# Attention scores from plain float32 queries and keys of 64 rows per head, in place of stacked high and low float32r parts

## The chip, the cores and the metric

One core of one Trainium2 chip runs the whole program in one launch. The metric is the time on the device in microseconds, the median of several runs.

## The reference

Three layers follow one another: attention over 4 batches x 8 heads (576 positions, 64 channels per head) with rotated queries and keys, a key/value layer with a gate, and a mixer over tokens and channels. What matters here is the first, cut to its core:

```python
def _attn_ref(q, k, v):                       # [4, 8, 576, 64]
    def rotate(x):
        x1, x2 = (x[..., :half], x[..., half:])
        return np.concatenate([x1 * cos - x2 * sin, x1 * sin + x2 * cos], axis=-1)
    q_rot, k_rot = (rotate(q), rotate(k))
    scores = scale * np.matmul(q_rot, k_rot.transpose(0, 1, 3, 2))     # scale = 1/8
    scores = scores - np.max(scores, axis=-1, keepdims=True)
    attn = np.exp(scores)
    attn = attn / (np.sum(attn, axis=-1, keepdims=True) + 1e-09)
    return np.matmul(attn, v).astype(np.float32)
```

The two layers behind it are products with weights w_k, w_v and w_r (the key/value and gate part) and w_tok1, w_tok2, w_ch1 and w_ch2 (the mixer).

## The kernel before

Heads are taken in pairs, A and B: 16 pairs in all, the 64 channels of A on partitions 0 to 63 and those of B on 64 to 127. A pair has nine score tiles, `TILES`: four of 128 queries for A, four for B, and R with the last 64 queries of both. Each tile has 576 scores per query, in two halves of 288 columns. 144 steps (`a_step`) go through the tiles one by one, in a pipeline: scores of tile i+1 on TensorE (`emit_S`), its maximum on VectorE (`emit_max`, L389), exponential of tile i on ScalarE (`emit_exp`, L396), then division into a high float16 part on ScalarE (`emit_hi`, through L75) and a low one on VectorE (`emit_lo`, L420), a transpose by DMA (`emit_tr`, L436 to L444) and the products with the values (`emit_pv`, L455), four units per pair. The score tiles have two buffers in PSUM (`S_p`).

`prep` does the work for the pairs to come, beside the steps: it loads keys and queries (`ld_raw`, L262, six buffers) and the values, rotates keys and queries on GpSimd in place (`rope`, two multiplications with the table `tab` and an addition; the first pair partly on VectorE), and scales the values (`v_max` to `v_shift`; its small products `vps` at L316 and L337 are plain float32, one row or one column wide, one call of each per pair).

TensorE takes float32r at a coarser precision than float32, so operands come in two parts: a high one, rounded, and a low one, the rest. For the scores `split_hi` copies the rounded keys and queries (the latter with the factor 1/8) on ScalarE (L73 and L75), and `split_lo` subtracts: keys on GpSimd (L297, through the helper at L104), queries on VectorE (L301). The two parts of the keys of one head are stacked on 128 partitions (`kst`: high on one half, low on the other), and each part of the queries stands on both halves (`qst`), which a DMA at L305 brings about (a ScalarE copy for the first pair). So one product over 128 rows does two of the four partial products, and a score tile takes four products (two parts of the queries, two halves of the columns); tile R, which takes both heads into one accumulation with zeros beside them, takes eight.

In the first four pairs VectorE also converts weights of the next layer (`Conv`, L201 to L207); from the fifth on the key/value products of the batch before (`kvr_gen`, `mm3`, L569 to L571, tiles kp and vp, 288 columns) run beside attention, ten of them per step (`KVN`, twice). The rest of that layer, the gate and the mixer come behind attention. The order on each engine is made by a scheduler from the program's order and the priorities in `PRI`; all DMAs are issued by SyncE.

Of the kernel before, what the change touches and what calls it, by code (L numbers as in the profile page):

```python
# [19 lines left out]
QW = 640  # L20
# [4 lines left out]
# float64 words as float32: the high word of float32's least and largest exponents  # L25
F64_LEAST = struct.unpack("<f", struct.pack("<I", 0x38000000))[0]
F64_MOST = struct.unpack("<f", struct.pack("<I", 0x47EFFFFF))[0]
# score tiles of a pair of heads: 128 queries of A or B; R: the last 64 of both
TILES = ["A0", "A1", "A2", "A3", "R", "B2", "B3", "B0", "B1"]
NT = len(TILES)  # L30
# steps, relative to a pair's first, of its four units of attention times value
PV_AT = {7: (0, 0), 10: (0, 1), 12: (1, 0), 13: (1, 1)}
# key/value and gate parts that run beside one another once attention is done with all but the last batch
SEQ = [("K", 3, 0), ("R", 0, 0), ("R", 0, 1), ("K", 3, 1)]
# how far each stream of work is taken at a time
KVN, TKN, PRE, PRE_EARLY, PRE_FROM = 5, 6, 20, 6, 6
# buffers of the pools of the first part
BUFS = dict(raw=6, vr=2, v16=2, e=7, p16=3, pt0=1, pt1=2, tm=2, sm=4, sc=3, la=1, lf=1, xs=4, t=2, q=2, vt=2)
# how much earlier than in the program's order the scheduler takes a kind of work
# [25 lines left out]
def body(tc, qk, vw, tabs, ident, mu, w_k, w_v, w_r, w_t1, w_t2, w_c1, w_c2, out):  # L65
# [18 lines left out]
    class ahead:  # L84
        """earlier (or, below 0, later) in the scheduler's order than in the program's"""
# [21 lines left out]
    with ctx:  # L107
# [10 lines left out]
        # ---------------------------------------------------------------- key/value/gate work and weights  # L118
# [7 lines left out]
        class Weights:  # L126
            """pieces of weights in a pool: each one's float64 words, then in their place its two float32r parts"""
# [28 lines left out]
        def behind(o, name):  # L156
            """keeps an instruction behind the latest of that name in their engine's order"""
            if name in last:
                tc.add_manual_dep(o.ins, last[name].ins.name, mybir.DependencyInfo(
                    mybir.DependencyClass.NoSync, mybir.DependencyReason.DATA), reason="order")  # L160

        class Conv:
            """splits weights piece by piece; the stages of successive pieces overlap"""
# [50 lines left out]
            def step(self):  # L214
                """two pieces further"""
                n = self.n
                self.n += 2
                with ahead(PRI.get(self.name, 0)):
                    for j in (3, 2, 1, 0):
                        for fs in zip_longest(*(self.stage(j, n + d - 2 * j) for d in range(2))):  # L220
                            for f in fs:
                                if f is not None:
                                    f()

        # ---------------------------------------------------------------- attention
# [11 lines left out]
        st_p = right("st", 1)  # L237
# [10 lines left out]
        tab = tab_p.tile([128, 2, S], F32, name="tab")  # L248

        raw_t, v_t, v16_t, sc_t = {}, {}, {}, {}  # L250
        # per head: [high; low] parts of the keys (low; high for the second), the queries' parts on both halves
        kst = [st_p.tile([128, S], F32R, name=f"kst{x}") for x in range(2)]
        qst = [st_p.tile([128, 2, QW], F32R, name=f"qst{x}") for x in range(2)]
# [20 lines left out]
        def rope(g, j, k, e):  # L274
            t = raw_t[g][j]
            if k < 2:
                o = tt(e, t[k], t[k], tab[:, k], ALU.mult)
# [4 lines left out]

        @prio("qk")
        def split_hi(g, x, j, e):
            l = slice(64 * x, 64 * x + 64)
            t = raw_t[g][j][0][l]
            if j == 0:
                copy(e, kst[x][l], t)
            else:
                copy(e, qst[x][l, 0, 64 * x:64 * x + S], t, 0.125)  # L290

        @prio("qk")
        def split_lo(g, x, j, e="P"):
            l, o = slice(64 * x, 64 * x + 64), slice(64 - 64 * x, 128 - 64 * x)
            t = raw_t[g][j][0][l]
            if j == 0:
                tt(e, kst[x][o], t, kst[x][l].bitcast(F32), ALU.subtract)  # L297
                return
            c = slice(64 * x, 64 * x + S)
            lo, hi = qst[x][l, 1, c], qst[x][l, 0, c].bitcast(F32)  # L300
            dve.scalar_tensor_tensor(out=lo, in0=t, scalar=0.125, in1=hi, op0=ALU.mult, op1=ALU.subtract)  # L301
            if g == 0:
                copy("A", qst[x][o, :, c], qst[x].bitcast(F32)[l, :, c])
            else:
                sp.dma_start(qst[x].bitcast(F32)[o, :, c], qst[x].bitcast(F32)[l, :, c])  # L305
# [14 lines left out]
        def v_pow(g):  # L320
            """a power of two that brings the values near float16's largest, and what undoes it"""
# [48 lines left out]
        def emit_S(i):  # L370
            n = TILES[i % NT]
            p = S_p.tile([128, 2, 512], F32, tag="S", name="S")
            parts = []
            for x, nm in enumerate("AB"):
                if n == "R":
                    parts.append((x, 512 if x == 0 else 0))
                elif n[0] == nm:
                    parts.append((x, 128 * int(n[1]) + 128 * x))
            for j, (x, c) in enumerate(parts):
                for s in range(2):  # L380
                    for h in range(2):
                        pe.matmul(p[:, h, 0:HS], lhsT=qst[x][:, s, c:c + 128], rhs=kst[x][:, h * HS:(h + 1) * HS],  # L382
                                  start=(j == 0 and s == 0), stop=(j == len(parts) - 1 and s == 1))
# [63 lines left out]
        def emit_pv(g, x, u):  # L447
            """the products; returns what follows on ACT and then on DVE"""
# [32 lines left out]
        def prep(g, k):  # L481
            """work for pair g; k: step relative to the first of pair g - 1"""
# [25 lines left out]
            if k in (4, 8):  # L508
                x = k // 8
                split_hi(g, x, 0, "A")  # L510
                split_hi(g, x, 1, "A")
            elif k in (5, 9):
                x = k // 9
                split_lo(g, x, 1)
                split_lo(g, x, 0)
# [4 lines left out]
        def a_step(i, kv):  # L520
            """one step of the attention's pipeline"""
# [31 lines left out]
        # ---------------------------------------------------------------- key/value part, gate part  # L553
# [12 lines left out]
        def mm3(p, w, m, t, first, last):  # L566
            """the products of w's m-th 128 columns"""
# [5 lines left out]
        def kvr_gen(seq, ready):  # L573
            """seq: list of (kind, b, c); kind K: key and value products, kind R: gate and its product"""
# [112 lines left out]
        # ================================================================ emission  # L687
        ld_raw(0, ((0, 0),))
        sp.dma_start(tab[:, 0], tabs[:, 0])
        ld_raw(0, ((1, 0), (0, 1)))  # L690
        sp.dma_start(tab[:, 1], tabs[:, 1])
        ld_raw(0, ((1, 1),))
# [5 lines left out]
        for x in range(2):  # L698
            pool.memset(qst[x].bitcast(F32)[:, :, S - S * x:QW - S * x], 0.0)
# [6 lines left out]
        for x in range(2):  # L706
            for j in (1, 0):
                split_hi(0, x, j, "A")
                split_lo(0, x, j, "D")
            if x == 0:  # L710
                emit_S(0)
                emit_max(0)
# [39 lines left out]
        def tok_gen(b):  # L752
            """u = y + token mixing, in place of y; half of the channels at a time"""
# [43 lines left out]
        # ---- second weights  # L797
# [40 lines left out]
        # ---------------------------------------------------------------- gate and mixer  # L838
# [9 lines left out]
        def gate_gen(b):  # L848
            """y = sigmoid(r) * v, in place of v"""
# [148 lines left out]
```

## Time and profile before

| | |
|---|---|
| median of 3 runs | 1056.97 us (1056.59 to 1060.08) |
| span of the profiled execution | 1055.4 us, 1.6 us under the median |
| TensorE (PE) busy | 879.1 us, 83% |
| VectorE (DVE) busy | 709.2 us, 67% |
| ScalarE (ACT) busy | 534.9 us, 51% |
| GpSimd (POOL) busy | 509.1 us, 48% |
| mean granted TensorE clock | 0.918 |
| attention | the first 525 us |

The shares are means over stages with different bounds, so a change in one stage is read from the stretch it lies in. A busy TensorE is counted with the pipeline of its matmuls: two that overlap count until the second has ended.

### The profile page before, as it was taken

To read this page: it belongs to the slowest core of one execution; us is meant where nothing else is said; L and a number is where in the kernel's file an instruction comes from. 1 tells how busy PE (TensorE), PEld (TensorE's weight loads), DVE (VectorE), ACT (ScalarE), POOL (GpSimd) and SP (SyncE) were. 2 spreads that over 40 slices of the span, in tenths; PEclk is the share of its full clock that TensorE was granted. 3 is DMA by queue.
4 is the path that set the end of the run, shared out by engine and by line. 5 is a ranking of instruction groups with operands and counts; after the bars stand their busy time and mean duration, and the time that the engine had idled before them with its cause. 6 is when DMAs were issued, how large, how long until landed. Compare 5 with 4: busy or idle time off the path is not lost.

```text
span 1055.4 us, 16829 instructions
## 1 busy us (share of the span) xinstructions
PE 879.1 (83%) x6000; PEld 814.4 (77%) x6000; DVE 709.2 (67%) x1355; ACT 534.9 (51%) x1130; POOL 509.1 (48%) x480
## 2 busy tenths in 40 slices
PE   2354566888887897788977898889999999999998
PEld 1333345677777787677967897889999999999997
DVE  6999999898899998998798459963222312131111
ACT  3665758777776786778754254443224112211110
POOL 6765885695889774774355545451123003201010
PEclk9665668999999999899988998989999999999999
DMA  6897979999897888979880147001021002000000
GB/s 199 206 204 184 214 168 189 184 203 191 181 185 172 185 187 175 202 140 197 200 272 17 42 171 284 16 24 46 1 85 30 23 1 73 1 24 1 24 23 23
DMA packets 216371, 130.56 MB, mean 124 GB/s; under 512 B 175712, under 2 KB 191200, under 8 KB 216160
## 3 DMA queue, kind: packets, MB, share of 16 engines
q1 hardware_dynamic: 216288, 129.50, 52.1%
q8 instruction: 47, 0.77, 0.3%
q14 instruction: 36, 0.29, 0.1%
HBM read 59.79 MB, written 14.16 MB: 70 GB/s over the span
## 4 chain that ended last, share of the span: by engine, by line
PE 37%; DVE 9%; issue 2%; DMA 1%; ACT 1%; POOL 1%; SPq 0%; DVEq 0%; POOLq 0%; ACTq 0%
PE c1p L569 4%; PE co L570 4%; PE co L569 4%; PE co L571 4%; PE c1p L570 4%; PE c1p L571 4%; DVE cv L201 2%; DVE cv L205 2%; DVE cv L207 1%; PE rp L569 1%; PE rp L570 1%; PE rp L571 1%; DVE cv L203 1%; PE trp L762 1%; PE t1p L776 1%
## 5 line engine op out<-in xcount | busy, mean ns | idle before, releaser
L382 PE MATMUL S<-kst,qst 128*128 128x288 f32 x640 | 136.0, 350 | 57.3 <-ACT e L396 44.1
L382 PEld LDWEIGHTS S<-kst,qst 128*128 128x128 f32 x640 | 110.3, 226 | 70.0 <-ACT e L396 49.4
L420 DVE SCALAR_TENSOR_TENSOR p<-e,rc,p 128x576 f16<-128x576 f32 x144 | 156.2, 1090 | 11.3 <-ACT p L75 10.8
L902 DVE SCALAR_TENSOR_TENSOR hs<-c1p,hs 128x288 fp32r<-128x288 f32 x96 | 43.5, 454 | 151.1 <-ACT hs L901 150.6
L75 ACT ACTIVATE p<-e,rc 128x576 f16<-128x576 f32 x144 | 110.1, 771 | 65.2 <-DMA pt<-p 30.8
L455 PE MATMUL pv<-pt,v 128*128 128x256 f16 (+1 forms) x576 | 97.2, 317 | 39.3 <-DMA pt<-p 34.6
L396 ACT ACTIVATE e<-S,nm 128x576 f32<-128x576 f32 x144 | 105.8, 735 | 44.5 <-DVE nm L389 43.3
L104 POOL TENSOR_TENSOR raw<-raw,tab 128x576 f32<-128x576 f32 x62 | 103.4, 1677 | 48.1 <-DMA raw<-in_qk_dram 47.8
L901 ACT ACTIVATE hs<-c1p 128x288 fp32r<-128x288 f32 x96 | 38.7, 408 | 170.0 <-PE c1p L571 166.4
L104 POOL TENSOR_TENSOR uhl<-y,uhl 128x288 fp32r<-128x288 f32 x32 | 25.8, 836 | 194.1 <-ACT uhl L73 194.1
L569 PE MATMUL c1p<-uhl,parts 128*128 128x288 f32 x384 | 116.0, 303 | 3.6 <-DVE hs L902 3.0
L571 PE MATMUL c1p<-uhl,parts 128*128 128x288 f32 x384 | 115.0, 300 | 0.1
L570 PE MATMUL c1p<-uhl,parts 128*128 128x288 f32 x384 | 114.9, 300 | 0.0
L570 PE MATMUL co<-hs,parts 128*128 128x288 f32 x384 | 113.3, 297 | 0.0
L571 PE MATMUL co<-hs,parts 128*128 128x288 f32 x384 | 113.0, 297 | 0.0
L389 DVE TENSOR_REDUCE nm<-S 128x1 f32<-128x576 f32 x144 | 107.2, 745 | 6.2 <-PE S L382 5.1
L569 PE MATMUL co<-hs,parts 128*128 128x288 f32 x384 | 109.7, 300 | 0.7 <-ACT hs L901 0.5
L455 PEld LDWEIGHTS <-v 128*128 128x128 f16 x576 | 55.4, 106 | 65.6 <-issue 29.5
L104 POOL TENSOR_TENSOR parts<-cv,parts 128x512 fp32r<-128x512 f32 (+2 forms) x51 | 73.5, 1441 | 56.8 <-ACT parts L73 54.5
L569 PE MATMUL kp<-xs,parts 128*128 128x288 f32 x256 | 80.5, 322 | 13.2 <-ACT vt L73 6.9
L569 PE MATMUL vp<-k,parts 128*128 128x288 f32 x256 | 78.2, 312 | 3.1 <-DVE k L80 1.5
L570 PE MATMUL kp<-xs,parts 128*128 128x288 f32 x256 | 79.4, 311 | 0.3 <-POOL xs L104 0.2
(111 smaller groups left out, 2527.8 us busy)
## 6 DMA issues: line engine op xcount, KB each, us to landing
raw<-in_qk_dram SPq DMA_DIRECT2D x64, 288.0 KB, 4.0
words<-in_w_c_dram SPq DMA_DIRECT2D x24, 512.0 KB, 8.3
qst<-qst SPq DMA_DIRECT2D x30, 288.0 KB, 3.7
vr<-in_vw_dram SPq DMA_DIRECT2D x16, 320.0 KB, 4.0
xd<-xT SPq DMA_DIRECT2D x16, 288.5 KB, 2.8
vd<-vt SPq DMA_DIRECT2D x32, 144.0 KB, 2.4
y<-vd SPq DMA_DIRECT2D x8, 576.0 KB, 5.7
out_dram<-y SPq DMA_DIRECT2D x8, 576.0 KB, 3.5
```

The lines of the kernel that those rows point to most:

```text
L75: act.activation(out=o, in_=i, func=AF.Copy, scale=scale)
L104: return (pool if e == "P" else dve).tensor_tensor(o, a, b, op=op)
L382: pe.matmul(p[:, h, 0:HS], lhsT=qst[x][:, s, c:c + 128], rhs=kst[x][:, h * HS:(h + 1) * HS], start=(j == 0 and s == 0), stop=(j == len(par ...
L389: dve.tensor_reduce(out=nm, in_=S_t[i][:, :, 0:HS], op=ALU.max, axis=AX.XY, negate=True)
L396: act.activation(out=e, in_=S_t.pop(i)[:, :, 0:HS], func=AF.Exp, bias=sum_t[i][:, 0:1], accum_out=s)
L420: dve.scalar_tensor_tensor(out=t[:, S:2 * S], in0=e_t.pop(i), scalar=sum_t.pop(i)[:, 0:1], in1=t[:, 0:S], op0=ALU.mult, op1=ALU.subtract)
L455: pe.matmul(p[:, 0:n], lhsT=vt[:, j, 128 * x:128 * x + 128], rhs=t[:, j, :], start=(j == 0), stop=(j == 8))
L569: pe.matmul(p, lhsT=wh, rhs=t[:, 0], start=first, stop=False)
L570: pe.matmul(p, lhsT=wh, rhs=t[:, 1], start=False, stop=False)
L571: pe.matmul(p, lhsT=wl, rhs=t[:, 0], start=False, stop=last)
L901: act.activation(out=h[:, 0], in_=p[:, 0:HS], func=AF.Relu)
L902: dve.scalar_tensor_tensor(out=h[:, 1], in0=p[:, 0:HS], scalar=0.0, in1=h[:, 0].bitcast(F32), op0=ALU.max, op1=ALU.subtract)
```

## The change

The queries and keys are no longer split. After the rotation, which now brings the factor 1/8 into the queries by a second pair of tables, a score product takes the 64 rows of a head as they are, in float32. A tile takes two products, R four (64 queries of A to the upper half of the output, 64 of B to the lower). `split_hi`, `split_lo`, `kst` and `qst` go, with the DMA between the halves and the memory they took; the loads have ten buffers in place of six, since keys and queries are now read until their pair's last tile. The table at the start is twice as large and is loaded in two parts, that for the keys first. All else is as before (the rest of the diff takes out comments).

```diff
-BUFS = dict(raw=6, ...
+BUFS = dict(raw=10, ...
...
-        st_p = right("st", 1)
-        tab = tab_p.tile([128, 2, S], F32, name="tab")
+        tab = tab_p.tile([128, 4, S], F32, name="tab")
-        kst = [st_p.tile([128, S], F32R, name=f"kst{x}") for x in range(2)]
-        qst = [st_p.tile([128, 2, QW], F32R, name=f"qst{x}") for x in range(2)]
...
-                o = tt(e, t[k], t[k], tab[:, k], ALU.mult)
+                o = tt(e, t[k], t[k], tab[:, 2 * j + k], ALU.mult)
...
-        def split_hi(g, x, j, e):
...
-        def split_lo(g, x, j, e="P"):
...
         def emit_S(i):
             n = TILES[i % NT]
             p = S_p.tile([128, 2, 512], F32, tag="S", name="S")
-            parts = []
+            g = i // NT
+            k, q = raw_t[g][0][0], raw_t[g][1][0]
             for x, nm in enumerate("AB"):
                 if n == "R":
-                    parts.append((x, 512 if x == 0 else 0))
+                    c, w, o = (512, 64, 0) if x == 0 else (0, 64, 64)
                 elif n[0] == nm:
-                    parts.append((x, 128 * int(n[1]) + 128 * x))
-            for j, (x, c) in enumerate(parts):
-                for s in range(2):
-                    for h in range(2):
-                        pe.matmul(p[:, h, 0:HS], lhsT=qst[x][:, s, c:c + 128], rhs=kst[x][:, h * HS:(h + 1) * HS],
-                                  start=(j == 0 and s == 0), stop=(j == len(parts) - 1 and s == 1))
+                    c, w, o = 128 * int(n[1]) + 64 * x, 128, 0
+                else:
+                    continue
+                l = slice(64 * x, 64 * x + 64)
+                for h in range(2):
+                    pe.matmul(p[o:o + w, h, 0:HS], lhsT=q[l, c:c + w], rhs=k[l, h * HS:(h + 1) * HS],
+                              start=True, stop=True)
...
-            if k in (4, 8):
-                x = k // 8
-                split_hi(g, x, 0, "A")
-                split_hi(g, x, 1, "A")
-            elif k in (5, 9):
-                x = k // 9
-                split_lo(g, x, 1)
-                split_lo(g, x, 0)
...
-        sp.dma_start(tab[:, 0], tabs[:, 0])
-        ld_raw(0, ((1, 0), (0, 1)))
-        sp.dma_start(tab[:, 1], tabs[:, 1])
-        ld_raw(0, ((1, 1),))
+        sp.dma_start(tab[:, 0:2], tabs[:, 0:2])
+        ld_raw(0, ((0, 1), (1, 0), (1, 1)))
+        sp.dma_start(tab[:, 2:4], tabs[:, 2:4])
...
-        for x in range(2):
-            for j in (1, 0):
-                split_hi(0, x, j, "A")
-                split_lo(0, x, j, "D")
-            if x == 0:
-                emit_S(0)
-                emit_max(0)
+        emit_S(0)
+        emit_max(0)
```

## Rows read from the trace of the kernel before

**Rows 1.** The page's 40 slices: busy tenths of VectorE.
```profile
DVE  6999999898899998998798459963222312131111
```
**Rows 2.** Stretches: start:end, length, busy us of each engine, clock, DMA share, GB/s.
```profile
25.00:150.00 125.00, 60.46 (x240) 44.31 (x239) 123.91 (x217) 79.23 (x149) 86.41 (x68) 0.64 0.86 197
150.00:525.00 375.00, 315.54 (x2127) 278.80 (x2127) 337.40 (x692) 283.79 (x583) 259.00 (x230) 0.94 0.90 184
500.00:525.00 25.00, 25.00 (x194) 23.68 (x193) 19.80 (x49) 19.93 (x44) 10.47 (x13) 1.00 0.88 184
525.00:575.00 50.00, 38.05 (x223) 34.70 (x222) 48.88 (x78) 25.13 (x55) 28.91 (x28) 0.83 0.50 168
700.00:1055.00 355.00, 350.27 (x2660) 348.81 (x2659) 89.38 (x200) 81.48 (x208) 52.52 (x67) 1.00 0.09 28
```
**Rows 3.** Timeline of PE (start, length, instruction): four score products in the stream.
```profile
463.93 0.70 PE L382 MATMUL S<-kst,qst 128*128 128x288 f32 x4
464.46 0.30 PE L569 MATMUL vp<-k,parts 128*128 128x288 f32 x1
```
**Rows 4.** Stretches again, score tile S alone: PE, PEld, DVE, ACT, clock, DMA.
```profile
25.00:150.00 125.00, 37.67 (x130) 29.57 (x129) 21.78 (x30) 23.88 (x58) 0.64 0.86 197
150.00:525.00 375.00, 94.17 (x496) 76.96 (x496) 83.41 (x112) 92.78 (x226) 0.94 0.90 184
```
**Rows 5.** Groups by line and shape, 150 to 525 us: the pv products.
```profile
L455 PE MATMUL pv<-pt,v 128*128 128x320 f16 x234 | 39.2, 310 | 16.6 <-DMA pt<-p 12.1 <-DVE p L420 2.4 <-DVE nm L389 0.9
L455 PE MATMUL pv<-pt,v 128*128 128x256 f16 x243 | 35.5, 290 | 6.8 <-DMA pt<-p 6.6 <-DVE rc L408 0.2
```
**Rows 6.** Timeline of PE around two pairs of small float32 products.
```profile
458.25 0.38 PE L316 MATMUL vps<-idn,vm 128*1 128x128 f32 x2 [3.40 <-DVE xT L472]
458.56 0.40 PE L569 MATMUL kp<-xs,parts 128*128 128x288 f32 x1
...
467.70 0.45 PE L455 MATMUL pv<-pt,v 128*128 128x320 f16 x2
468.08 0.38 PE L337 MATMUL vps<-vb,ones 1*128 1x2 f32 x2
468.39 0.40 PE L570 MATMUL vp<-k,parts 128*128 128x288 f32 x1
```
**Rows 7.** Groups by line over the run: busy us, mean ns, idle before.
```profile
L104 POOL TENSOR_TENSOR kst<-raw,kst 64x576 fp32r<-64x576 f32 x30 | 49.3, 1644 | 30.4 <-ACT kst L73 28.4 <-PE pv L455 0.4
L73 ACT ACTIVATE kst<-raw 64x576 fp32r<-64x576 f32 x32 | 21.4, 668 | 7.9 <-DVE raw L104 7.8
L420 DVE SCALAR_TENSOR_TENSOR p<-e,rc,p 128x576 f16<-128x576 f32 x144 | 156.2, 1090 | 11.3 <-ACT p L75 10.8
```
**Rows 8.** Waits, 150 to 525 us: who for whom, total us, times, longest.
```profile
PE pv L455 <- DMA pt<-p: 18.7, 13, 3.4
DVE nm L389 <- PE S L382: 4.4, 6, 1.4
```
**Rows 9.** Groups by line, DVE, from 25 to 150 us and from 150 to 525 us.
```profile
L301 DVE SCALAR_TENSOR_TENSOR qst<-raw,qst 64x576 fp32r<-64x576 f32 x6 | 9.0, 1504 | 0.1
L301 DVE SCALAR_TENSOR_TENSOR qst<-raw,qst 64x576 fp32r<-64x576 f32 x24 | 30.3, 1263 | 0.4
```
**Rows 10.** Instructions of tile p: duration ns least/median/most, first and last start.
```profile
L420 DVE SCALAR_TENSOR_TENSOR p<-e,rc,p x144: 787/820/2051, 26.2 to 521.7; 128x576 f16<-128x576 f32 x144
```
**Rows 11.** Timeline of the start: the addition that ends the rotation, the first scores.
```profile
11.08 1.97 DVE L104 TENSOR_TENSOR raw<-raw 128x576 f32<-128x576 f32 x1
19.92 2.29 PE L382 MATMUL S<-kst,qst 128*128 128x288 f32 x8 [8.21 <-ACT qst L73]
```
**Rows 12.** Instructions of tile vps, as in rows 10.
```profile
L316 PE MATMUL vps<-idn,vm x32: 269/272/421, 11.1 to 458.4; 128*1 128x128 f32 x32
```
**Rows 13.** Timeline of PE around two transposes of 64 columns in the last stage.
```profile
724.06 0.38 PE L762 MATMUL trp<-idn,y 128*64 128x128 f32 x2
...
724.42 0.30 PE L570 MATMUL c1p<-uhl,parts 128*128 128x288 f32 x1
```

## What I expect of the change, and why

> **What bounds the kernel now.** I read the page's slices first [rows 1]: VectorE (DVE) is mostly at 80% and more in the first 20 of 40 slices, that is in the attention stage, and falls to 10 to 30% in the last third. The table by stretches [rows 2] then cuts the span into stages. From 25 to 150 us DVE is busy 123.9 of 125 us: weight conversion and attention share it, and it is the bound; TensorE (PE) runs at a granted clock of 0.64 there, a mix of its two levels 1.2 and 2.4 GHz. From 150 to 525 us DVE is busy 337.4 of 375 (90%) and PE 315.5 (84%) at clock 0.94. From 525 to 575 DVE (weight conversion) is the bound, and from 700 on PE (350 of 355 us). The change touches nothing behind 525 us, so all of its gain or loss has to arise in the first half.
>
> The busy share of PE overstates its load, since a matmul is recorded with its pipeline (about 0.30 us) while the next starts earlier. So I counted PE by starts. Four score products take from 463.93 to 464.46 us [rows 3], 0.133 us each at full clock. From 150 to 525 us there are 2127 products [rows 2]: 496 are scores, for 112 tiles (one maximum on DVE each) [rows 4], 477 are pv (attention times value) [rows 5], some 46 are the small vps (four a call, twelve calls), and the other 1108 are kp and vp, of the key/value part, with 288 columns like the scores. With 0.133 us for 288 columns, 0.14 for 320 (two pv take 0.45, one 0.31 [rows 5, 6]) and 0.118 for 256 in proportion, that is 66 us of scores, 147 of kp and vp, 62 of pv and about 12 of vps (1 us a call, below): 287 us, 77% of the stretch. The last 25 us of it hold 194 products and PE at 25.00 of 25 us, DVE at 19.8 [rows 2]: PE can be kept full beside attention, and then it sets the pace.
>
> **What the change removes.** Per pair of heads two DVE subtractions (L301) for the low part of the queries, two GpSimd (POOL) subtractions for that of the keys, four ScalarE (ACT) copies and two DMAs between halves of the partitions (L305). Over the run POOL loses 49.3 us and ACT some 43 (the key copies have 21.4 [rows 7], the queries' are as many and as large). ACT is busy 76% and POOL 69% of the stretch from 150 to 525 us [rows 2], so what they save I cost at nothing: DVE and PE, fuller than both, cover it; if that cover went, it would be worth those sums. SyncE's queue loses the DMAs, which wait there for DVE with transposes behind them; nothing again, since PE has work of the key/value part in the meantime, and the gain is bounded by the 18.7 us in which PE waited for transposes in that stretch [rows 8]. DVE gets back 9.0 us between 25 and 150 us and 30.3 between 150 and 525 [rows 9]. Its p subtraction takes 0.79 us at the least, 0.82 in the middle, but 1.09 in the mean [rows 7, 10]: it is stretched at times, plausibly by POOL. If a tenth of POOL's work goes, I give DVE another 2 us before 150 and 5 after; the bounds are 0 and the whole excess, 144 x 0.27 = 39 us.
>
> At the start the first scores begin at 19.92 us, while the queries' rotation is done at 13.05 [rows 11]; what lies between is splitting. The tables are doubled, though (128 rows x 1152 words more, 590 KB), and at the 197 GB/s of the next stretch [rows 2] that is 3 us ahead of the rotation: I take 4 of the 7 us, bounds 1 and 7.
>
> **What it adds.** Per score tile two products of 64 rows in place of four of 128 (four in place of eight for tile R). But they are plain float32. The trace has such products in vps: 16 calls leave 32 matmul records, and two with 128 columns take 0.38 us together where one takes 0.27 [rows 6, 12], so the second ends 0.11 us behind the first, that is 128 columns at two cycles of 2.4 GHz each. A plain float32 product is thus two passes at half rate, four times a float32r one. With 288 columns: 2 x 0.24 us. The number of passes stays at 496 in the stretch, each 0.24 in place of 0.133 us: 119 for 66 us, 53 more.
>
> The second cost is the small tile. The vps products use part of the array (one row, or one column). Around the one at 468.08 us PE is not in its stride: the last pv slot ends near 467.98 (467.70 + 2 x 0.14), the load of the weights starts only at 468.08, the next full product is recorded at 468.39 but takes 0.40 instead of 0.30 us, so it streams from 468.49 [rows 6]. That is 0.51 us for a pair that streams two columns, and two such calls (vps has two kinds) make the 1 us above; taking off its second load (0.11, as the second product of the pair at 458.25 comes [rows 12]), which longer products would cover, 0.40 us is lost around it. The one at 458.25 had waited anyway and loses only the exit: 458.56 + 0.10 less two passes of 0.11, 0.20 us. I put 0.40 us, the row whose stream goes on before and behind, on each of the 112 score tiles; bounds 0.20 (PE idle before it anyway) and 0.52. That is 45 us. Nothing in the trace shows a tile of 64 rows, so this is the weakest term. The Trainium skill, "TensorEngine Tiling (Array Packing)", Key Properties, says that a change of tiling mode drains the engine; 64 rows would be such a mode, and by that rule the term stands, without it the 45 us are zero.
>
> **The sum.** From 150 to 525 us PE would need 287 + 53 + 45 = 385 us at full clock where the stretch has 375, while DVE falls to 302. PE becomes the bound. With 98% of the time used (the last 25 us show full use) the stretch takes 393 us, 18 more. From 25 to 150 us PE had 240 products, 130 of them scores [rows 2, 4]. If the clock stays at the lower level these cost 130 x 0.48 + 30 tiles x 0.5 + 110 others x 0.24 = 104 us, against 124 - 11 = 113 left for DVE: it fits, but closely, and I take 9 of the 11 us. The late score (some 1 us longer per tile at half clock) holds up the maximum on DVE, and behind that every DVE instruction; the maximum waited on scores only 4.4 us in 375 [rows 8], so there is room. What is moved besides (the loads' buffers, ten for six) meets no queue that is shorter than before, and I cost it at nothing; its cover is the pair of lead that the loads have. Together: 1055.4 - 4 - 9 + 18 = 1060.4 for the span. The median of the runs, 1056.97, is 1.6 us above the profiled span, which I add: 1062 us.
>
> **Rivals.** (1) No loss at the small tiles: the drain belongs to one-row products and not to 64 rows. Then PE needs 340 us, at 95% 358: 17 saved, and 9 + 4 before; 1055.4 - 30 + 1.6 = 1027. For it speaks that two transposes of 64 columns run on in the stream, to the second product behind them 0.36 us have gone, which is their own two passes of 0.11 and one slot of 0.133 [rows 13]; against it that both kinds of vps show a loss, and that the transposes use all 128 rows. This is the other side: it decides from a loss of 0.36 us a tile down, where PE's sum is 380, the stretch 388 and the 13 us gained earlier are no longer used up.
> (2) The weight loads are exposed as well. Full-array loads run ahead under the stream, and the load of the second product at 458.25 did not hold that one up (0.11 us is its predecessor's stream). In 64-row tiles each further load would add 0.11 us, three per tile and seven for R: 112 x 0.37 = 42 us on top, (385 + 42)/0.98 = 436, so 1055.4 - 13 + 61 + 1.6 = 1105. The Trainium skill, "TensorE: Matmul & The Clock Gate", Part 3, The mechanism, has loads overlap running products only where the row group differs, which would give this; the row just named speaks against it.
> (3) Nothing moves: PE's loss is spent in its idle time (89 us by the count above) and the pace is set by the latency from scores through maximum, exponential and transpose, which gets longer by PE's share as DVE's gets shorter: about 1057. PE's waits of 18.7 us on the transposed pt [rows 8] show that this chain holds PE at times; that PE was full in the last 25 us speaks against it.
>
> **How the numbers follow.** A measurement of this kernel can tell about 0.3%, 3 us. Forecast (PE bound, loss around 0.40): 0.66; its own range 1037 (loss 0.25, full use: 368 us) to 1084 (loss 0.52, 96%: 415 us). It lies close to the old time, so of the 0.66 I put 0.40 on slower, 0.12 on same and 0.14 on faster. Rival 1: 0.20, nearly all faster. Rival 2: 0.08, slower. Rival 3: 0.06, mostly same. Faster 0.34, same 0.18, slower 0.48. The range runs from rival 1 (1024, a little under it) to a little above the forecast's upper end (1090); what lies beyond is most of rival 2, the low half of rival 1 and some of the forecast's ends, just under 0.2.
>
> **What would show it.** The score passes must stand 0.24 us apart at full clock; if 0.12, the change gains some 40 us and I am wrong at the root. A kp product recorded right behind a score tile should take 0.40 us and come about 0.2 late (loss there) or not (rival 1). The stretch to the last score should show PE at over 95% and clock near 1.00, DVE near 77%; if DVE stays at 90% and the stage is shorter, rival 1 holds. The first score should begin near 16 us. From the end of attention on, times should only be shifted; if that part changes, the order of the work has changed and not only its cost.

## The result, and the profile after

The changed kernel takes 1069.92 us in the median of five runs (1063.54 to 1071.66) where the kernel before takes 1056.97: the ratio is 1.0092, with a 95% interval of 1.0064 to 1.012. It is slower by about 1%, some 8 us more than forecast (1062), inside the range and on the side that was given the largest chance. The profiled execution is the fastest of the five, 1063.54 us with a span of 1061.7, so the traces compare 1055.4 with 1061.7: 6.3 us. One run of the kernel before took 1141.98 us, in the slower of the chip's two states, and is left out of the ratio.

The stretches of the kernel after (columns as in [rows 2]; the four lines answer to its first four):

```profile
25.00:150.00 125.00, 85.73 (x257) 45.48 (x253) 120.36 (x215) 70.56 (x133) 82.04 (x68) 0.70 0.76 181
150.00:525.00 375.00, 360.86 (x2060) 263.57 (x2060) 303.01 (x660) 256.37 (x532) 199.15 (x196) 0.98 0.81 168
500.00:525.00 25.00, 25.00 (x169) 20.73 (x168) 17.89 (x41) 19.11 (x43) 7.58 (x9) 1.00 0.79 186
525.00:575.00 50.00, 38.09 (x244) 34.97 (x242) 47.63 (x77) 23.27 (x52) 34.76 (x32) 0.93 0.38 119
```

From 150 to 525 us TensorE (PE) went from 315.5 to 360.9 us busy (96%) and its granted clock from 0.94 to 0.98; VectorE (DVE) fell from 337.4 to 303.0, GpSimd (POOL) from 259 to 199. PE does less in that time: 2060 products where there were 2127. The bound has moved from DVE to PE.

A wait from 150 to 525 us says the same (engine, line, what it waited for: us, times, longest):

```profile
DVE nm L363 <- PE S L356: 18.3, 28, 1.5
```

The maximum on DVE waits 18.3 us for scores where it waited 4.4 [rows 8]: DVE is now behind PE.

The score products themselves, in PE's stream, first a tile of one head, then the first two of its four passes by themselves, then a tile R:

```profile
307.49 0.29 PE L536 MATMUL vp<-k,parts 128*128 128x288 f32 x1
307.71 1.23 PE L356 MATMUL S<-raw 64*128 64x288 f32 x4
308.87 0.40 PE L537 MATMUL vp<-k,parts 128*128 128x288 f32 x1
309.11 0.29 PE L535 MATMUL vp<-k,parts 128*128 128x288 f32 x1
...
307.71 0.51 PE L356 MATMUL S<-raw 64*128 64x288 f32 x1
308.06 0.40 PE L356 MATMUL S<-raw 64*128 64x288 f32 x1
...
228.91 1.19 PE L356 MATMUL S<-raw 64*64 64x288 f32 x8 [0.29 <-ACT e L370]
```

The vp product before the first tile streams until 307.49 + 0.133 = 307.62. The next one is recorded at 308.87 with 0.40 in place of 0.29 us, and its successor starts at 309.11, so it streams from 309.11 - 0.133 = 308.98. The tile has taken 1.36 us. Its four passes of 0.242 us are 0.97 us in all, so 0.39 us is lost around them. Like the vp product behind the tile, the first pass is recorded 0.1 us too long (0.51 us, the others 0.40), and the second starts 0.35 us behind it; so the first streams from 308.06 - 0.24 = 307.82, and the last, which starts at 308.54, until 308.78. So some 0.20 us is lost ahead of the passes and as much behind. The tiles that stand in the stream of kp and vp agree to 0.02 us (36 of them, median 1.36). The kernel before has 0.53 us there in the median and loses nothing (27 tiles). The second tile was not in the forecast: R has eight records and takes no longer than a tile of four. Its products for head A and for head B start 13 ns apart and run side by side; in the stream of kp and vp such a tile takes 1.32 us.

### The profile page after: what moved, and what is told of

Same layout as the page of the kernel before. It is cut to its first block, busy times and chain, and to the rows that moved or that the text cites. A ratio compares the mean times of both kernels' runs of the same rounds, so it can differ in the third digit from the quotient of the medians.

```text
span 1061.7 us, 16551 instructions
## 1 busy us (share of the span) xinstructions
PE 960.7 (90%) x6000; PEld 807.8 (76%) x6000; DVE 668.5 (63%) x1321; ACT 497.3 (47%) x1064; POOL 449.7 (42%) x448
## 4 chain that ended last, share of the span: by engine, by line
PE 52%; DVE 9%; DMA 2%; issue 2%; ACT 1%; POOL 1%; SPq 0%; DVEq 0%; ACTq 0%; POOLq 0%
PE S L356 5%; PE c1p L535 4%; PE co L536 4%; PE co L537 4%; PE co L535 4%; PE c1p L536 4%; PE c1p L537 4%; PE pv L429 2%; DVE cv L204 2%; DVE cv L200 2%; PE kp L535 2%; PE vp L536 2%; PE kp L536 1%; DVE cv L206 1%; PE kp L537 1%
## 5 line engine op out<-in xcount | busy, mean ns | idle before, releaser
L356 PE MATMUL S<-raw 64*128 64x288 f32 (+1 forms) x640 | 203.5, 481 | 37.5 <-ACT e L370 35.1
L356 PEld LDWEIGHTS S<-raw 64*128 64x128 f32 (+1 forms) x640 | 107.7, 200 | 98.7 <-ACT e L370 53.2
L394 DVE SCALAR_TENSOR_TENSOR p<-e,rc,p 128x576 f16<-128x576 f32 x144 | 150.5, 1048 | 13.5 <-ACT p L74 12.6
L103 POOL TENSOR_TENSOR raw<-raw,tab 128x576 f32<-128x576 f32 x62 | 98.1, 1594 | 76.6 <-DMA raw<-in_qk_dram 74.6
L429 PE MATMUL pv<-pt,v 128*128 128x256 f16 (+1 forms) x576 | 100.0, 319 | 15.8 <-DMA pt<-p 8.3
L103 POOL TENSOR_TENSOR parts<-cv,parts 128x512 fp32r<-128x512 f32 (+2 forms) x51 | 78.3, 1537 | 64.3 <-ACT parts L72 62.1
L103 POOL TENSOR_TENSOR k<-q,k 128x288 fp32r<-128x288 f32 x56 | 50.8, 911 | 90.0 <-DVE k L79 47.9
L535 PE MATMUL kp<-xs,parts 128*128 128x288 f32 x256 | 79.7, 317 | 5.2 <-ACT t L596 2.6
```

Of the source, the lines that this page charges most:

```text
L103: return (pool if e == "P" else dve).tensor_tensor(o, a, b, op=op)
L356: pe.matmul(p[o:o + w, h, 0:HS], lhsT=q[l, c:c + w], rhs=k[l, h * HS:(h + 1) * HS], start=True, stop=True)
L394: dve.scalar_tensor_tensor(out=t[:, S:2 * S], in0=e_t.pop(i), scalar=sum_t.pop(i)[:, 0:1], in1=t[:, 0:S], op0=ALU.mult, op1=ALU.subtract)
L429: pe.matmul(p[:, 0:n], lhsT=vt[:, j, 128 * x:128 * x + 128], rhs=t[:, j, :], start=(j == 0), stop=(j == 8))
L535: pe.matmul(p, lhsT=wh, rhs=t[:, 0], start=first, stop=False)
```

## Where the 6.3 us come from

Three marks in the two traces divide the span: the first score, the start of the fifth pair (the 161st score product) and the last score. The score tile after, and the last products of the key/value part before (first line) and after:

```profile
L356 PE MATMUL S<-raw x640: 402/403/846, 14.1 to 516.4; 64*128 64x288 f32 x128, 64*64 64x288 f32 x32
```
```profile
L569 PE MATMUL vp<-k,parts x256: 290/295/642, 214.5 to 637.1; 128*128 128x288 f32 x128
```
```profile
L535 PE MATMUL vp<-k,parts x256: 291/295/442, 216.4 to 642.2; 128*128 128x288 f32 x128
```

| from, to | before, us | after, us | difference |
|---|---|---|---|
| start, first score | 19.92 | 14.10 | -5.8 |
| first score, fifth pair | 145.3 | 144.9 | -0.4 |
| fifth pair, last score | 351.2 | 357.4 | +6.2 |
| last score, last vp | 120.7 | 125.8 | +5.1 |
| last vp, end | 418.3 | 419.5 | +1.2 |

Attention ends at 516.4 us in both. But in the kernel before 1068 of the 1536 key/value products (kp and vp) are done by then, in the one after 1019: 49 are left for later. So the fourth line is the bill for the third, and PE's slowdown costs 6.2 + 5.1 = 11.3 us, of which the early start has paid 5.8.

## Experiments

### Does the splitting matter, and does the loss at a tile?

e3 takes the high parts alone (float32r, no splitting) and mixes both heads over all 128 rows; e2 does the same with 64 rows per head; e7 issues each product of e3 twice, so that PE has the load of the kernel before, and e8 three times. Keys and queries get a rounded tile `rr` from the addition of the rotation, and the loads go back to six buffers; both set these kernels apart from the change too (the lines of e3; e2 keeps the 64 rows, e7 and e8 have a loop around the product):

```diff
-o = tt(e, t[0], t[0], t[1], ALU.add)
+rr_t[g, j] = rr_p.tile([128, S], F32R, tag="rr", name="rr")
+o = tt(e, rr_t[g, j], t[0], t[1], ALU.add)
...
-pe.matmul(p[o:o + w, h, 0:HS], lhsT=q[l, c:c + w], rhs=k[l, h * HS:(h + 1) * HS], start=True, stop=True)
+pe.matmul(p[:, h, 0:HS], lhsT=q[:, c:c + 128], rhs=k[:, h * HS:(h + 1) * HS], start=True, stop=True)
```

> The changed kernel with rotated queries and keys rounded to float32r and the score products in float32r (the low parts are left out; R takes 128 queries of one head). Tiles of 64 rows stay, the passes fall from four of 0.24 us to two of 0.133 per tile. Theory: 0.27 us of passes and still about 0.40 us lost around them, so TensorE saves 0.69 us a tile, 6 us a pair; DVE, with 25 us of work a pair, becomes the bound again, a pair takes 26 to 27 us and the run 1020 us (1010 to 1030). Rival (latency sets the pace): 1050 or more.

> As the one with float32r and 64 rows, but over all 128 rows (heads mixed, low parts left out): neither the passes nor the change of tile are left, so this is what taking the splitting away is worth by itself. Theory: DVE is the bound, 25 us of work a pair, so little below the 64-row form: 1015 us (1005 to 1025). If the loss around a tile still counted there, it would be 20 us or more below it.

> Splitting gone as in the changed kernel, but TensorE with just the score passes of the kernel before: float32r over 128 rows (heads mixed, low parts left out), each product issued twice, 0.53 us a tile as before. So it shows what taking the splitting away is worth while TensorE does what it did. Theory (DVE was the bound, and what it is relieved of is time): 1003 to 1012 us, as with half the passes (1008). Rival (much of the 5% of the float32r forms is the passes that they spare TensorE, 38 us over the run): 1030 or more.

> The same with each product issued three times, 0.80 us of TensorE a tile, between the float32r form with 64 rows (0.66 with its loss, 1003 us) and the float32 one with 128 rows (0.97, 1062 and, with zero rows, 1050). Theory (TensorE takes over as the bound where its work per pair, 17.4 us and ten times that of a tile, passes the 25 us of DVE): here 25.4 against 25, so just at the knee, 1015 to 1030. Rival (float32 passes cost by themselves, whatever their length): 1003 to 1012 still.

Measured: e2 1003.52 us, ratio 0.9488 (0.9463 to 0.9512); e3 1007.94 us, 0.9531 (0.9506 to 0.9557); e7 1020.82 us, 0.9634 (0.96 to 0.9669); e8 1029.36 us, 0.973 (0.9684 to 0.9775). e3 and e8 came as expected; e2 was faster than its range, and e7 lies between its theory and its rival. The stretch from 150 to 525 us of e2, e3 and e7:

```profile
150.00:525.00 375.00, 338.63 (x2080) 276.25 (x2078) 334.49 (x713) 266.48 (x567) 241.41 (x227) 0.92 0.86 181
```
```profile
150.00:525.00 375.00, 315.61 (x2040) 273.03 (x2040) 333.28 (x711) 264.80 (x564) 238.82 (x225) 0.91 0.85 181
```
```profile
150.00:525.00 375.00, 323.83 (x2234) 287.30 (x2235) 322.55 (x691) 261.98 (x557) 229.69 (x220) 0.96 0.83 180
```

e7 leaves PE's load as it was and takes 39 us off. Not all of that need be the splitting: e7 also has the tiles `rr` and an order of its own, which may be worth 12 us of it (e1 and e4, below). Which engine's share of it counts, e7 doesn't separate, since ACT and POOL lose their parts too; DVE was the fullest of the three [rows 2], and in e2 and e3 it is busy 89% beside attention. Here is e2's tile in the stream:

```profile
304.16 0.30 PE L540 MATMUL vp<-k,parts 128*128 128x288 f32 x1
304.39 0.53 PE L361 MATMUL S<-rr 64*128 64x288 f32 x2
304.85 0.40 PE L541 MATMUL vp<-k,parts 128*128 128x288 f32 x1
305.08 0.29 PE L542 MATMUL vp<-k,parts 128*128 128x288 f32 x1
```

From 304.16 + 0.133 to 305.08 - 0.133 are 0.65 us for two passes of 0.133: again 0.39 us lost, with another type and another pass length. The e3 tiles lose nothing. Yet e2 is no slower than e3: PE, recorded as 84 to 90% busy with its pipeline, has idle time in both, and the loss does not show in the time.

### What do the passes cost, and what the loss, in float32?

e1 keeps the change's float32 but takes 128 rows, mixing both heads (a tile R is then 128 queries twice). It has the passes without the loss. e9 is e1 with half again as many products (the first half of the columns is done twice), e5 the change with one table, which brings the root of 1/8 to both sides, so that the 590 KB more at the start are gone.

```diff
-l = slice(64 * x, 64 * x + 64)
...
-pe.matmul(p[o:o + w, h, 0:HS], lhsT=q[l, c:c + w], rhs=k[l, h * HS:(h + 1) * HS],
+pe.matmul(p[:, h, 0:HS], lhsT=q[:, c:c + 128], rhs=k[:, h * HS:(h + 1) * HS],
```

> The changed kernel with its float32 score products taken over all 128 rows, so that the two heads of a pair are mixed in the scores (R: 128 queries, twice); passes, columns and all other work as in the changed kernel. Only the change of tile between 64 and 128 rows is gone. Theory (TensorE is the bound from 150 us on, and each score tile costs it 0.40 us around its passes): the loss around a score tile goes to zero, a pair of heads takes 28 to 29 us in place of 30.7, and the run 1040 us (1030 to 1050). Rival (the pace is set by the latency from scores to transposes, TensorE's loss lies in its waits): 1060 or more, with TensorE idle for as much longer.

> Float32 over 128 rows (heads mixed) with the first half of the scores done again, three products a tile: 1.45 us of TensorE in the stream, no change of tile, against 0.97 and its loss of 0.39 in the changed kernel, 1.36. Theory (a loss around a tile is time of TensorE like any other): as the changed kernel or a little slower, 1066 to 1080. Rival (the loss hides where streams do not): clearly slower than the changed kernel, 1085 or more.

> The changed kernel with one pair of tables that carry sqrt(1/8), for keys and queries alike, so 590 KB less are loaded at the start. By cost alone this is worth at most 3 us, at the start. It also makes the scheduler order the work anew, so a difference of more than 3 us from the changed kernel is what another order is worth by itself. Theory that order decides within some 10 us: 1056 to 1076. Theory that orders are alike: 1064 to 1068.

Measured: e1 1061.61 us, 1.0029 (1.0004 to 1.0054); e9 1119.18 us, 1.0565 (1.0532 to 1.0597); e5 1071.42 us, 1.0114 (1.009 to 1.0139). e1 was expected at 1040 us and came out in the range of its rival; e9 is slower than its theory had it (1066 to 1080). e1's stretch, then e9's:

```profile
150.00:525.00 375.00, 346.33 (x2074) 285.69 (x2075) 301.03 (x669) 256.94 (x537) 196.52 (x196) 0.98 0.82 168
```
```profile
150.00:525.00 375.00, 350.51 (x1987) 283.03 (x1987) 273.22 (x598) 231.92 (x471) 176.06 (x173) 1.00 0.71 147
```

Without the loss the passes alone bring e1 back to the time before: they use up nearly all that the splitting gave. With the loss, the change is 0.6% slower than e1, some 7 us. The larger table costs nothing that shows in the whole (e5's first scores begin at 13.2 us to 14.1, but its ratio of 1.0114 lies within the change's interval). e5 was also to show what another order is worth: here no more than these 0.2%, within the noise. e9 is 49 us slower than the change although its tile of one head takes 1.45 us to the change's 1.36. The expectation left out two things. Tile R takes 2.9 us in e9 and 1.3 in the change; and the change's 144 tiles stand in 122 runs without another product between, and a run pays the loss once (in one at 169.03 us all eight passes of two tiles start 0.24 us apart after the first). So over the whole PE spends 232 us on the scores of e9 and 187 on those of the change, which is 45 of the 49 us, and no hidden loss is needed to explain e9.

### The same comparison with one order

The scheduler orders each kernel anew, so e1 differs from the change in more than its rows. g1 and g2 take the program's own order, which is the same on every engine for both (the records agree one by one); g1 has float32 with 64 rows (R as 128 queries of one head, twice), g2 with 128.

```diff
-with _tile.TileContext(nc, schedule_with_timeline_sim=True) as tc:
+with _tile.TileContext(nc) as tc:
```

> The scheduler made a new order for every kernel so far, so the loss around score tiles has not yet been compared at one order. This kernel and its partner are ordered by the program's order and priorities, without the scheduler's timeline, which gives both the same order on every engine. This one has float32 products over 64 rows as in the changed kernel (R takes 128 queries of head A twice, so its scores are not those of the reference). Theory (a TensorE that is full pays each loss in time): slower than its partner with 128 rows by 0.39 us x 144 tiles x the share of steps in which TensorE sets the pace, 25 to 50 us. Rival (the losses fall into waits that the order has anyway): within 12 us of its partner.

> The partner: the same order on every engine, float32 products over 128 rows (heads mixed), so no change of tile. Theory: 25 to 50 us faster than the form with 64 rows; rival: within 12 us of it.

Measured: g1 1176.91 us, 1.1111 (1.1067 to 1.1154); g2 1148.1 us, 1.0847 (1.0824 to 1.087). The score tiles of g1 and g2:

```profile
L358 PE MATMUL S<-raw x640: 402/507/846, 14.2 to 579.1; 64*128 64x288 f32 x160
```
```profile
L357 PE MATMUL S<-raw x640: 403/406/849, 14.5 to 551.9; 128*128 128x288 f32 x160
```

The loss alone is worth 28.8 us here, within the range of the theory, and the last score shows 27.2 of them. This order puts other products between the halves of many tiles: the scores stand in 189 runs, not 144, which is why the median pass of g1 is one recorded with 0.51 us, the first of a run. So PE loses up to 189 x 0.39 = 74 us: some 40% reaches the time, the rest falls where PE would have waited. Both are far slower than the scheduled kernels, so the share is that of this order and need not be that of the change.

### A version that beats both

e4 keeps float32 and does without 64-row tiles: each head's queries stand in a tile of 128 rows whose other half was filled with zeros once, so the other head's keys add nothing. One table with the root of 1/8 serves both sides. e6 is e4 with eight key/value products per step in place of ten (`KVN` 4).

```diff
-o = tt(e, t[0], t[0], t[1], ALU.add)
+if j == 0:
+    kr_t[g] = kr_p.tile([128, S], F32, tag="kr", name="kr")
+    o = tt(e, kr_t[g], t[0], t[1], ALU.add)
+else:
+    for x in range(2):
+        l = slice(64 * x, 64 * x + 64)
+        o = tt(e, qz[g % 2][x][l, 64 * x:64 * x + S], t[0][l], t[1][l], ALU.add)
...
+pe.matmul(p[:, h, 0:HS], lhsT=qz[g % 2][x][:, c:c + 128], rhs=k[:, h * HS:(h + 1) * HS],
+          start=(m == 0), stop=(m == len(parts) - 1))
```

> A complete form without the change of tile: the rotated queries of each head are written into a tile of 128 rows whose other half stays zero (two buffers per head, one more GpSimd addition of 1.6 us a pair), the score products are float32 over all 128 rows, and one pair of tables with the factor sqrt(1/8) serves keys and queries. Theory: like the full-row form with mixed heads, 1038 us (1028 to 1050), about 2% below the kernel before, since GpSimd has the room. Rival (latency): 1060 or more. If GpSimd's added work counted, it would be 10 us or more above the mixed form.

> The zero-filled complete form with four key/value products in place of five at a time beside attention (KVN = 4). TensorE is fuller in attention than behind it, where weight conversion on DVE holds it up and it is 76% busy. Theory (TensorE's work sets the pace in attention): attention ends some 20 us earlier and half of that is given back behind it: 1040 us against 1050 (1034 to 1046). Rival (order or latency sets the pace): attention ends no earlier and the run takes 1052 or more.

Measured: e4 1049.55 us (1044.57 to 1050.31), 0.9914 (0.9879 to 0.9948); e6 1049.76 us, 0.9916 (0.9886 to 0.9947). e4 is 20 us faster than the change and 9 faster than the kernel before in the same comparison (1059.79 us). e4's stretch:

```profile
150.00:525.00 375.00, 342.67 (x2082) 284.75 (x2083) 318.88 (x671) 254.81 (x530) 234.84 (x224) 0.98 0.82 170
```

PE has the same score passes as in e1 (155 us over the run) and the clock is the same, yet e4 is 12 us faster than e1. They differ in the buffers of the rotation, in one more addition on POOL per pair and in the order; which of these makes the 12 us was not separated. The marks show where the lead begins: the first four pairs, with DVE busy 95% in both, take 132.8 us in e4 and 144.6 in e1. At the last score the two are level, with 20 more key/value products done in e4, and at the last of these e4 is 13.7 us ahead. All kernels of the scheduler that write the rotated keys and queries to tiles of their own take 125 to 134 us there (e2, e3, e4, e6, e7, e8), and all whose products read them where they were rotated 144.6 to 151.6 (the change, e1, e5, e9). PE's load does not sort them: e1 has that of e4. Under the program's own order g2, which reads them in place, takes 134.1, so the tiles are not the only thing that can do it. e6 is inconclusive: the scheduler placed as many products beside attention as before (1004 key/value products by the last score in both), so the edit did not bring about what it was to test; attention ends at 508.7 us to 508.2.

### The splitting's other half on another engine

e10 leaves the kernel before as it is, but moves the queries' low part from DVE to POOL (the tables bring the root of 1/8, so that a plain subtraction does):

```diff
-dve.scalar_tensor_tensor(out=lo, in0=t, scalar=0.125, in1=hi, op0=ALU.mult, op1=ALU.subtract)
+tt(e, lo, t, hi, ALU.subtract)
```

> The kernel before in all (split, stacked float32r, 0.53 us of TensorE a tile), but the low part of the queries is taken on GpSimd in place of DVE, which the factor sqrt(1/8) in the tables of keys and queries makes possible. DVE is relieved of 42 us, GpSimd gets 52 more. Theory (DVE is the bound of attention, GpSimd at 69% has room): 1040 us (1025 to 1050). Rival (the two engines stretch one another, as DVE's p subtraction with a mean of 1.09 and a least of 0.79 us suggests, or GpSimd's queue becomes the bound): 1053 or more.

Measured: 1069.41 us, 1.0091 (1.0061 to 1.0121). It was to gain, and lost 10 us. The p subtraction and the stretch in e10:

```profile
L420 DVE SCALAR_TENSOR_TENSOR p<-e,rc,p x144: 786/1072/2074, 26.7 to 524.0; 128x576 f16<-128x576 f32 x144
```
```profile
150.00:525.00 375.00, 303.83 (x2060) 265.67 (x2061) 332.81 (x662) 278.30 (x573) 294.29 (x255) 0.95 0.90 180
```

The 30.3 us of [rows 9] are gone from DVE, but it is still busy 332.8 us to 337.4: the median p subtraction went from 0.82 [rows 10] to 1.07 us while POOL went from 259 to 294 us in that stretch. So here DVE was stretched as POOL worked more. The Trainium skill, "Perfetto Trace Analysis", Optimizing Scalar/DVE Operations, says that the two share a read port, so that work moved between them may not help; the trace agrees, with 0.25 us on the median subtraction. With DVE as busy as before there was no gain to be had. The loss shows in the key/value part: the last score is 1 us later than before (517.6 us), but 1044 kp and vp products are done by then, to 1068. Which wait makes it so was not separated.

### The scheduled runs on one scale

| kernel | splitting | PE for the scores, us | median, us |
|---|---|---|---|
| e3 | no | 43 | 1007.9 |
| e7 | no | 85 | 1020.8 |
| e2 | no | 86 | 1003.5 |
| e8 | no | 128 | 1029.4 |
| e4, e6 | no | 155 | 1049.6, 1049.8 |
| e1 | no | 155 | 1061.6 |
| change, e5 | no | 187 | 1069.9, 1071.4 |
| e9 | no | 232 | 1119.2 |
| before | yes | 85 | 1057.0 |
| e10 | yes, on POOL | 85 | 1069.4 |

The third column is passes times 0.133 or 0.242 us, over 128 tiles of one head and 16 R, plus 0.39 per run of score products where there is a loss (122 runs in the change, 123 in e5, 111 in e2). Up to about 130 us the times lie between 1003 and 1029, not in the order of PE's load, which decides little there. Kernels with the same load, or nearly, stand up to 17 us apart (e1 and e4, e2 and e7); as every kernel is ordered anew, some of that may be the order, and its size stays open. From 155 on the time rises with PE's load, from e1 and e4 (mean 1055.6) to e9 by 63.6 us for 77, that is 0.83 us for each, but not evenly: the change lies 12 us under that line. By the ratios it is made of -3.7% (39 us) up to e7, and of +4.6% (49 us) from e7 to the change, which has 102 us more of PE. Up to 12 us of both may belong to the tiles of the rotation and the order (e1 and e4), so the splitting was worth 27 to 39 us and PE's scores cost 37 to 49.

## Why the prediction was right, step by step

- **DVE is the bound before, and PE would be after.** PE at 96% with DVE waiting on scores shows the second; for the first, e7 shows that the splitting took 27 to 39 us, though not that all of them were DVE's.
- **Two passes per float32 product, 0.24 us each.** Right: 0.242 us each, from the 0.11 us of the 128-column products [rows 6].
- **0.40 us lost around a 64-row tile**, called the weakest term: right, 0.39 us in the change and 0.39 in e2. The row that was chosen, the one whose stream goes on before and behind, was the fitting one. Rival 1 (no loss) falls with it. The rule of the Trainium skill that the prediction cites from "TensorEngine Tiling (Array Packing)", Key Properties, that a change of tiling mode drains the engine, holds here, with that price. e2's equal loss in another type and pass length, and the lack of one in e1 and e3, tie it to the 64 rows. The count was a little high: the tiles from 150 to 525 us stand in 105 runs, so it is at most 41 us and not 45.
- **The loads of the weights are hidden.** Right, and rival 2 falls: passes of 64 rows stand at 0.242 us with loads of 0.187 us (the median of 640) between them. By the rule of the Trainium skill that the prediction cites from "TensorE: Matmul & The Clock Gate", Part 3, The mechanism, they would stand further apart; the trace does not bear it out.
- **496 passes of 0.24 in the stretch, +53 us.** The count was right, and so was the price of a pass alone, but not that of all. Each of some twelve tiles R in the stretch takes its eight passes in the time of four, 0.97 us less than counted: 12 us too much in the sum. The diff shows the reason, had it been read for it: A's 64 queries stand in other rows and other columns of the array than B's (rows 0 to 63 and output 0 to 63, rows 64 to 127 and output 64 to 127). The Trainium skill, "TensorEngine Tiling (Array Packing)", Key Properties, says that different tiles run in parallel; the trace agrees, with eight products in 1.19 us where four take 1.23.
- **The stretch: +18 us.** Measured 11.3 (third and fourth line of the table above). With 12 us less for R and 4 less for the loss the sum would be (385 - 16) / 0.98 = 377, that is +2; the other 9 us are not settled (the granted clock of 0.98, where the sum has full speed, could be up to 0.02 x 375 = 8 of them).
- **The start: -4 us, bounds 1 and 7.** Measured -5.8: the first score begins at 14.10 us, not 16. It follows the rotation at once, which ends one us later than before [rows 11]:

```profile
12.11 1.94 DVE L103 TENSOR_TENSOR raw<-raw 128x576 f32<-128x576 f32 x1 [0.60 <-POOL raw L103]
14.10 4.20 PE L356 MATMUL S<-raw 64*128 64x288 f32 x8 [1.95 <-DVE raw L103]
```

- **25 to 150 us: -9 us.** This failed: the first four pairs take 144.9 us to 145.3. The 9.0 us of [rows 9] left DVE, but its other instructions grew. Two of the conversions and the p subtraction from 25 to 150 us, before and then after:

```profile
L420 DVE SCALAR_TENSOR_TENSOR p<-e,rc,p 128x576 f16<-128x576 f32 x28 | 30.5, 1092 | 0.1
L205 DVE SCALAR_TENSOR_TENSOR cv<-words,cv 128x512 int32<-128x512 int32 x16 | 16.8, 1052 | 0.0
L207 DVE SCALAR_TENSOR_TENSOR cv<-words,cv 128x512 int32<-128x512 int32 x16 | 14.6, 910 | 0.0
```
```profile
L394 DVE SCALAR_TENSOR_TENSOR p<-e,rc,p 128x576 f16<-128x576 f32 x28 | 32.1, 1150 | 0.0
L206 DVE SCALAR_TENSOR_TENSOR cv<-words,cv 128x512 int32<-128x512 int32 x16 | 18.5, 1153 | 0.0
L204 DVE SCALAR_TENSOR_TENSOR cv<-words,cv 128x512 int32<-128x512 int32 x16 | 18.2, 1137 | 0.0
```

  The conversions took 36.7 us to 31.4 and the p subtraction 32.1 to 30.5, for the same counts: 6.9 us back. DVE's idle time grew from 1.1 to 4.6 us, 3.5 more, behind the later scores among others. That is more than the 9.0 saved. Two us of relief from POOL were forecast in its place; POOL was busy 82.0 us to 86.4, so its total doesn't explain what grew. Nor does PE's load: e1 and e4 have the same, and the first four pairs take 144.6 us in e1 and 132.8 in e4, 129.3 in e7. So there was a gain to be had without the splitting, and the change, which reads keys and queries in place with ten load buffers (cost at nothing in the prediction), did not get it; whether these or the order held it back stays open.
- **Relief of DVE from POOL: 2 us before 150, 5 behind.** All p subtractions together take 150.5 us to 156.2 [rows 7], 5.7 less; since those from 25 to 150 us grew by 1.6, it is 7.3 less behind 150. The second half of the term held, the first had the wrong sign.
- **DVE in the stretch: 302 us.** It is 303.0, 81% of it.
- **PE's loss in idle time (rival 3).** It has a part in it: of up to 74 us lost, 28.8 reached the time at equal order, and none showed between e2 and e3, where PE had idle time. From 185 to 480 us PE waited for the transposed pt 14.5 us before, 4.5 after and 11.3 in e1: as the loss goes, part of the waits come back.
- **Behind attention only shifted.** The last score stands where it stood, but the key/value products left over came on top; from the last vp on it is a shift, to 1.2 us.

So the forecast of the span, 1060.4 us, came within 1.3 us of the 1061.7 measured, but partly because errors cancel. Inside the stretch, R and the loss were put 16 us too high and some 9 were missing. The stretch as a whole was put 6.7 us too high and the early pairs' gain 8.6 too high, the start's 1.8 too low, and 1.2 came behind the key/value part. The median of the runs lies 8.2 us above the profiled span, where the forecast added 1.6, and this makes most of the 8 us by which it missed; no trace shows where those runs spend it.

## What to carry to other kernels

A float32 product saves splitting on the vector engines and pays two passes at about half rate on TensorE, so count TensorE's stream first; here the splitting was worth 27 to 39 us and the passes and tiles 37 to 49. Take full 128 rows where TensorE is near its bound: they gave 29 us at equal order, and a form with zeros in the unused half (e4) was 20 us faster than the change, 12 of which e1, with full rows too, did not have. Where two 64-row products have other rows and other columns, though, issue them one after the other: they run together.

## What the runs showed of the hardware

- A tile of 64 rows between products of 128 costs 0.39 us at full clock, about half of it ahead and half behind, with two passes of 0.133 us in it as with four of 0.242. It is paid once per run of such products: e2's R, four passes, takes 0.92 us where two take 0.65. With a pv product behind it, 0.10 us is lost there in place of 0.20 (28 runs of the change from 210 to 480 us: pv starts 0.34 us behind the last pass). Fewer and longer runs would pay the loss less often; a kernel made for that was not tried.
- Eight products of 64 rows by 64 columns, A and B by turns, take 1.19 us by their records, four of 64 by 128 take 1.23. Whether two tiles of one head each, A's and B's by turns into two buffers, would run together as well was not tried; it would be the next thing to do with the change.
- Moving 30 us of subtraction from DVE to POOL left DVE's busy time nearly as it was (332.8 to 337.4 us): the p subtraction's median rose from 0.82 to 1.07 us.
